# A retention layer feeding a two-layer network: the opening of the kernel written out by hand

## The chip, the cores and the metric
The kernel runs on one core of one Trainium2 chip. The metric is the device time of one execution in microseconds (us), lower is better. Three executions of the kernel before took 356.39, 356.45 and 356.95 us (median 356.45).

## What is computed
For 8 batches of 8 heads, 576 positions and 64 features per head, q, k and v come in as float32. First a retention layer (attention without a softmax, with a decay gamma per head), then two dense layers on 4608 tokens of 512 features:

```python
scores = (q @ k.T) / 8                          # per batch and head, 576 x 576
D[i, j] = gamma[h] ** (i - j) if i >= j else 0
x = (scores * D) @ v                            # heads side by side: 4608 x 512
h = x @ w_in                                    # 512 -> 2048
g = maximum(0.01 * h, h)                        # leaky relu
out = g @ w_out                                 # 2048 -> 512, float32
```

## The kernel before, in words
**Units.** The retention is cut into 40 units: five per batch, four of 128 positions and one of 64. A unit u needs three loads (`load`, L102: k, q and v, 256 KB each, 128 KB for a unit of 64), three casts to f16 (`cast`, L112: k on ACT, q and v scaled by powers of gamma on DVE, v on POOL from some unit on) and then three kinds of TensorE work, which `burst` (L138) issues together:
- `tr`: transposes of q and k (L159), copied out of PSUM as kT (ACT, L249) and qT (DVE or ACT, L250);
- `sc`: the products of k and q within chunks of 64 positions (L171) and the state products k^T v (L184). DVE masks the scores to s16 (L263) and adds the state up over the batch in s32 (L273 to L281, two or three instructions); a copy to f16 is st16 (ACT or POOL, L287);
- `ot`: the output, scores times v (L197) plus state times q (L212), copied to xT by ACT (L257). xT holds the transposed tokens for layer one.

One burst can hold `tr` of unit n, `sc` of unit n-1 and `ot` of unit n-2. Each engine executes its instructions in the order in which this Python code emits them (the schedule is manual), and each waits for its own operands.

**Tokens.** The 4608 tokens are cut into groups (`sizes`, L367): 256, 256, then eight of 512. `g1_blocks` (L388) gives the pieces of layer one of a group. A piece fills one PSUM tile `hps` (two buffers): 4 matmuls of 512 columns, or 8 of 256 in a group of 256, then one leaky relu on ACT (L407). `g2_blocks` (L414) gives layer two: per block of 128 tokens 16 matmuls of 512 columns into a PSUM tile `yps` (two buffers), in four parts of 4; after the last part DVE copies it out (L433) and SP stores it (L435).

**Order.** The units' work is a list of `steps`. `early(u)` (L331, units 0 to 3) casts, issues a burst with `tr` of u and `ot` of u-1, then a second burst with `sc` of u. `steady(n)` (L341) issues loads of unit n+4, then one burst `tr` n, `sc` n-1, `ot` n-2, then the casts of n+1. `run` (L443) emits the pieces of the given lists and spreads the steps between them; `ends[g]` says how many steps must have been emitted before group g. The main part (L454 to L461) emits seven steps up to `steady(5)` first, then layer one of groups 0 and 1 without steps, then layer two of both, two token blocks at a time, with steps 6 to 10 between, then layer one of group 2 with steps 11 to 14, and from there layer one of g alternating with layer two of g-1.

**Queues.** k of unit 0 is loaded through SP. All else in the opening goes through POOL's queue in this order: q and v of unit 0, units 1 to 3, four quarters of w_in (`load_w_in`, cast to f16 by the DMA), unit 4, four quarters of w_out, then units 5 to 8 as the steps come. From unit 9 loads go through SP, in one queue with the stores of the output. t32, the landing buffers of the loads, has five buffers for each of q, k and v.

Of the kernel before, what the change touches and what calls it, by code (L numbers as in the profile page):

```python
# [9 lines left out]
FP = mybir.dt.float32  # L10
# [7 lines left out]
def kernel(  # L18
# [21 lines left out]
    nc = tc.nc  # L40
    B, H, S, D = q.shape
    NT, DM = out.shape
    DFF = moe_w_in.shape[1]
    P = 128
# [3 lines left out]
    NF = DFF // P  # L48
# [24 lines left out]
    o_pool = ctx.enter_context(tc.tile_pool(name="op", bufs=4))  # L73
# [4 lines left out]
    h_pool = ctx.enter_context(tc.tile_pool(name="hpp", bufs=2, space=PSUM))  # L78
    y_pool = ctx.enter_context(tc.tile_pool(name="yp", bufs=2, space=PSUM))
# [13 lines left out]
    w_out16 = const_pool.tile([P, NF, DM], F16, name="w_out16")  # L93

    units = [(b, w) for b in range(B) for w in range((S + P - 1) // P)]
    NU = len(units)
    nrows = [min(P, S - P * w) for b, w in units]
    EARLY = 4
    t32 = {}
    t16 = {}  # L100

    def load(u, x, eng):  # L102
        b, w = units[u]
        n = nrows[u]
        t = ld_pool.tile([P, H, D], FP, name=f"t32_{x}")
        t32[u, x] = t
        eng.dma_start(
            out=t[0:n],
            in_=(q, k, v)[x][b, :, P * w : P * w + n, :].rearrange("h t d -> t h d"),
        )  # L110

    def cast(u, x):  # L112

        b, w = units[u]
        n = nrows[u]
        t = a_pool.tile([P, H, D], F16, name=f"t16_{x}")
        t16[u, x] = t
        if x == 1:
            nc.scalar.copy(out=t[0:n], in_=t32[u, x][0:n])  # L119
        else:  # L120
            eng = nc.gpsimd if (x == 2 and u >= EARLY + 2) else nc.vector
            eng.tensor_tensor(  # L122
                out=t[0:n],
                in0=t32[u, x][0:n],
                in1=tab_sb[0:n, w % 2, x // 2, :].unsqueeze(2).to_broadcast([n, H, D]),
                op=MUL,
            )
# [10 lines left out]
    def burst(tr=None, sc=None, ot=None):  # L138
# [106 lines left out]
        if tr is not None:  # L245
            n = nrows[tr]
            qTs[tr] = a_pool.tile([P, NP, P], F16, name="qT")
            kTs[tr] = a_pool.tile([P, NP, P], F16, name="kT")
            nc.scalar.copy(out=kTs[tr][:, :, 0:n], in_=tiles["tr"][:, 1, :, 0:n])  # L249
            (nc.vector.tensor_copy if tr < EARLY else nc.scalar.copy)(  # L250
                out=qTs[tr][:, :, 0:n], in_=tiles["tr"][:, 0, :, 0:n]
            )
        if ot is not None:
            b, w = units[ot]
            n = nrows[ot]
            t0 = b * S + P * w
            nc.scalar.copy(out=xT[:, :, t0 : t0 + n], in_=tiles["ot"][:, :, 0:n])  # L257
        if sc is not None:
            b, w = units[sc]
            n = nrows[sc]  # L260
            s16 = a_pool.tile([P, NP, 2, CH], F16, name="s16")
            s16s[sc] = s16
            nc.vector.tensor_tensor(  # L263
                out=s16[0:n].rearrange("s p h t -> s (p h) t"),
                in0=tiles["sc"][0:n].rearrange("s p h t -> s (p h) t"),
                in1=mask_sb[0:n].unsqueeze(1).to_broadcast([n, H, CH]),
                op=MUL,
            )
            if n == P:
                st = tiles["st"]  # L270
                s32 = a_pool.tile([P, 2, NP, CH], FP, name="s32")
                if w == 0:
                    nc.vector.tensor_copy(out=s32[:, 0], in_=st[:, 0])  # L273
                else:
                    nc.vector.tensor_tensor(out=s32[:, 0], in0=st[:, 0], in1=carry[b], op=ADD)
                if w % 2 == 0:
                    nc.vector.tensor_tensor(out=s32[:, 1], in0=st[:, 1], in1=s32[:, 0], op=ADD)  # L277
                else:
                    tmp = a_pool.tile([P, NP, CH], FP, name="stmp")
                    nc.vector.tensor_tensor(out=tmp, in0=st[:, 1], in1=s32[:, 0], op=ADD)  # L280
                    nc.vector.tensor_tensor(  # L281
                        out=s32[:, 1], in0=tmp,
                        in1=gblk_sb.unsqueeze(2).to_broadcast([P, NP, CH]), op=MUL,
                    )
                carry[b] = s32[:, 1]
                st16[sc] = a_pool.tile([P, 2, NP, CH], F16, name="st16")
                (nc.scalar.copy if sc < EARLY + 2 else nc.gpsimd.tensor_copy)(  # L287
                    out=st16[sc], in_=s32
                )

# [9 lines left out]
    def load_w_out(c):  # L300
        nc.gpsimd.dma_start(
            out=w_out16[:, 4 * c : 4 * c + 4, :],
            in_=moe_w_out[c * FQ : (c + 1) * FQ, :].rearrange("(c k) f -> k c f", k=P),
        )
# [5 lines left out]
    load(0, 1, nc.sync)  # L310
    load(0, 0, nc.gpsimd)
    load(0, 2, nc.gpsimd)
    for u in range(1, EARLY):
        for x in (1, 0, 2):
            load(u, x, nc.gpsimd)
    for c in range(4):
        load_w_in(c)
    for x in (1, 0, 2):
        load(EARLY, x, nc.gpsimd)
    for c in range(4):  # L320
        load_w_out(c)

    def casts(u):
        if u < NU:
            for x in (1, 0, 2):
                cast(u, x)


    steps = []

    def early(u):  # L331


        def go():
            casts(u)
            burst(tr=u, ot=u - 1 if u else None)
            burst(sc=u)

        steps.append((u - 1, go))

    def steady(n):  # L341
        def go():
            if EARLY + 1 <= n + 4 < NU:
                for x in (1, 0, 2):
                    load(n + 4, x, nc.gpsimd if n + 4 < EARLY + 5 else nc.sync)
            burst(
                tr=n if n < NU else None,
                sc=n - 1 if EARLY <= n - 1 < NU else None,
                ot=n - 2 if EARLY - 1 <= n - 2 else None,
            )  # L350
            casts(n + 1)

        steps.append((n - 2, go))

    def preload():
        for u in range(EARLY + 1, EARLY + 4):
            for x in (1, 0, 2):
                load(u, x, nc.gpsimd)
        casts(EARLY)

    for u in range(EARLY):
        early(u)
    steps.append((EARLY - 1, preload))
    for n in range(EARLY, NU + 2):
        steady(n)

    sizes = [256, 256] + [512] * 8  # L367
    starts = [sum(sizes[:g]) for g in range(len(sizes))]
    NG = len(sizes)
    ends = []  # L370
    for g in range(NG):
        last = max(
            u for u, (b, w) in enumerate(units) if b * S + P * w < starts[g] + sizes[g]
        )
        ends.append(1 + max(i for i, (u, f) in enumerate(steps) if u <= last))
    ends += [ends[-1]] * 2
    done = 0

    def run_steps(upto):
        nonlocal done  # L380
        while done < upto:
            steps[done][1]()
            done += 1

    g_tiles = {}
    y_cur = {}

    def g1_blocks(g):  # L388

        tok, t0 = sizes[g], starts[g]  # L390
        nf = TOK // tok

        def block(fb):
            if fb == 0:
                g_tiles[g] = g_pool.tile([P, NF, tok], F16, name=f"gt{tok}")
            hps = h_pool.tile([P, nf, tok], FP, name="hps")
            for f in range(nf):
                fc = fb * nf + f
                for c in range(NP):
                    nc.tensor.matmul(  # L400
                        out=hps[:, f, :],
                        lhsT=w_in16[:, c, fc * P : (fc + 1) * P],
                        rhs=xT[:, c, t0 : t0 + tok],
                        start=(c == 0),
                        stop=(c == NP - 1),
                    )
            nc.scalar.activation(  # L407
                out=g_tiles[g][:, fb * nf : (fb + 1) * nf, :], in_=hps,
                func=mybir.ActivationFunctionType.Lrelu,
            )  # L410

        return [lambda fb=fb: block(fb) for fb in range(NF // nf)]
# [30 lines left out]
    def run(upto, *lists):  # L443

        order = sorted(
            ((n + 0.5) / len(ls), x, n) for x, ls in enumerate(lists) for n in range(len(ls))
        )
        a = done
        for m, (_, x, n) in enumerate(order):
            lists[x][n]()  # L450
            run_steps(min(upto, a + -(-(upto - a) * (m + 1) // max(1, len(order) - 3)), done + 1))
        run_steps(upto)

    run_steps(ends[1])  # L454
    run(ends[1], g1_blocks(0))
    run(ends[1], g1_blocks(1))
    run(ends[2], g2_blocks(0, 2) + g2_blocks(1, 2))
    run(ends[3], g1_blocks(2))
    for g in range(3, NG):
        run(ends[g + 1], g1_blocks(g), g2_blocks(g - 1))  # L460
    run(ends[NG], g2_blocks(NG - 1))  # L461

# [29 lines left out]
```

## Time and profile before

| | |
|---|---|
| median of three runs | 356.45 us |
| the profiled execution | 356.42 us |
| its span in the profile | 354.4 us |
| PE busy (TensorE matmul) | 306.5 us, 86% |
| ACT busy (ScalarE) | 163.7 us, 46% |
| DVE busy (VectorE) | 112.7 us, 32% |
| POOL busy (GpSimd) | 89.4 us, 25% |
| data moved by DMA | 42.68 MB |

The span runs from the first to the last instruction that the profile shows; the device time holds some two microseconds more. PE busy counts pipelined matmuls by their modelled ends, so the shares are read by stretch, not as a mean.

### The profile page before, as it was taken

How to read it: one execution, taken by the hardware profiler on the slowest of the kernel's cores; microseconds unless marked ns; L12 is line 12 of the kernel's file. 1: busy time of each engine (PE TensorE's matmuls, PEld its weight loads, DVE VectorE, ACT ScalarE, POOL GpSimd, SP SyncE). 2: the span in 40 equal slices, each digit the busy share in tenths (PEclk: the TensorE clock that was granted, in tenths of full speed). 3: DMA queues.
4: the chain of work that ended last, by engine and by line, in shares of the span. 5: the costliest groups of instructions: out<-in, count | busy, mean ns of one | idle time of the engine just before them, and what ended most of it. 6: DMA issues, size and time to landing. Idle time of an engine off the chain costs nothing.

```text
span 354.4 us, 10218 instructions
## 1 busy us (share of the span) xinstructions
PE 306.5 (86%) x4544; PEld 159.7 (45%) x4544; DVE 112.7 (32%) x207; ACT 163.7 (46%) x307; POOL 89.4 (25%) x99
## 2 busy tenths in 40 slices
PE   1342089979889999999999999999999999999995
PEld 1232068544444544444454544444544444444442
DVE  1554030373551343234243424233343321100021
ACT  3233046553776564555465555554465533333300
POOL 8825341043432243022232223221303200000000
PEclk9999999999999999999999999999999999999999
DMA  8999999257995465268075565664620000010011
GB/s 177 213 208 195 222 216 206 62 135 136 225 204 115 103 137 120 76 157 172 32 166 120 135 138 128 125 151 105 153 60 31 31 31 31 30 59 31 30 77 71
DMA packets 98731, 42.68 MB, mean 120 GB/s; under 512 B 88416, under 2 KB 92512, under 8 KB 98688
## 3 DMA queue, kind: packets, MB, share of 16 engines
q1 hardware_dynamic: 92192, 31.33, 38.9%
q0 software_dynamic: 6208, 10.62, 15.8%
q8 instruction: 35, 0.57, 0.7%
q10 hardware_dynamic: 288, 0.08, 0.2%
q14 instruction: 8, 0.07, 0.1%
HBM read 36.78 MB, written 9.44 MB: 130 GB/s over the span
## 4 chain that ended last, share of the span: by engine, by line
PE 81%; DMA 5%; ACT 5%; DVE 4%; issue 3%; POOL 0%; ACTq 0%; POOLq 0%
PE hps L400 34%; PE yps L423 33%; DMA t<-in_q_dram 5%; PE tr L159 4%; PE st L184 3%; PE sc L171 2%; PE ot L197 2%; PE ot L212 2%; ACT t L119 1%; DVE s L263 1%; ACT xT L257 1%; ACT kT L249 1%; DVE t L122 1%; ACT qT L250 1%; ACT gt L407 1%
## 5 line engine op out<-in xcount | busy, mean ns | idle before, releaser
L400 PE MATMUL hps<-xT,w_in 128*128 128x512 f16 (+1 forms) x640 | 145.8, 361 | 2.5 <-ACT gt L407 2.5
L423 PE MATMUL yps<-w_out,gt 128*128 128x512 f16 x576 | 143.7, 379 | 0.0
L407 ACT ACTIVATE gt<-hps 128x512 f16<-128x512 f32 x144 | 86.0, 600 | 95.2 <-PE hps L400 94.2
L400 PEld LDWEIGHTS <-w_in 128*128 128x128 f16 x640 | 61.4, 99 | 61.5 <-issue 3.7
L423 PEld LDWEIGHTS <-gt 128*128 128x128 f16 x576 | 55.2, 98 | 65.0
L287 POOL CAST st<-s 128x512 f16<-128x512 f32 x27 | 26.6, 984 | 175.1 <-DVE s L277 92.1
L159 PE MATMUL tr<-ident,t 64*64 64x64 f16 x1152 | 38.6, 202 | 32.6 <-DVE t L122 31.2
L263 DVE TENSOR_TENSOR s<-sc,cs 128x512 f16<-128x512 f32 (+1 forms) x40 | 27.6, 690 | 104.8 <-PE sc L171 94.0
L433 DVE COPY osb<-yps 128x512 f32<-128x512 f32 x36 | 24.6, 689 | 105.0 <-PE yps L423 105.0
L159 PEld LDWEIGHTS <-t 64*64 64x64 f16 x1152 | 28.7, 114 | 48.9 <-DVE t L122 34.3
L249 ACT COPY kT<-tr 128x512 f16<-128x512 f16 (+1 forms) x40 | 21.7, 542 | 51.7 <-PE sc L171 24.9
L122 DVE TENSOR_TENSOR t<-t,cs 128x512 f16<-128x512 f32 (+1 forms) x46 | 31.2, 685 | 19.9 <-DMA t<-in_q_dram 18.7
L122 POOL TENSOR_TENSOR t<-t,cs 128x512 f16<-128x512 f32 (+1 forms) x34 | 35.1, 1039 | 3.8 <-PE hps L400 2.9
L119 ACT CAST t<-t 128x512 f16<-128x512 f32 (+1 forms) x40 | 25.3, 633 | 11.0 <-DMA t<-in_k_dram 11.0
L171 PE MATMUL sc<-qT,kT 64*64 64x64 f16 x576 | 26.1, 199 | 4.6 <-ACT xT L257 3.4
L197 PE MATMUL ot<-s,t 64*64 64x64 f16 x576 | 24.9, 200 | 1.0
L212 PE MATMUL ot<-qT,st 64*64 64x64 f16 x512 | 24.1, 199 | 0.1
L184 PE MATMUL st<-t,t 64*64 64x64 f16 x512 | 21.2, 204 | 3.2
L257 ACT CAST xT<-ot 128x512 f16<-128x512 f32 (+1 forms) x40 | 22.4, 561 | 1.3 <-PE ot L212 1.3
L171 PEld LDWEIGHTS <-kT 64*64 64x64 f16 x576 | 18.9, 113 | 5.0 <-ACT kT L249 3.3
L250 ACT COPY qT<-tr 128x512 f16<-128x512 f16 (+1 forms) x36 | 19.6, 544 | 0.0
L197 PEld LDWEIGHTS <-t 64*64 64x64 f16 x576 | 17.2, 112 | 2.8 <-issue 2.8
(21 smaller groups left out, 99.6 us busy)
## 6 DMA issues: line engine op xcount, KB each, us to landing
out_dram<-osb SPq DMA_DIRECT2D x36, 256.0 KB, 2.2
t<-in_k_dram SPq DMA_DIRECT2D x25, 256.0 KB, 4.4
t<-in_q_dram SPq DMA_DIRECT2D x24, 256.0 KB, 5.0
t<-in_v_dram SPq DMA_DIRECT2D x24, 256.0 KB, 5.1
t<-in_q_dram POOLq DMA_DIRECT2D x8, 256.0 KB, 8.6
t<-in_v_dram POOLq DMA_DIRECT2D x8, 256.0 KB, 8.5
w_in<-in_moe_w_in_dram POOLq DMA_DIRECT2D x4, 512.0 KB, 12.4
w_out<-in_moe_w_out_dram POOLq DMA_DIRECT2D x4, 512.0 KB, 15.0
```

Source lines behind the costliest of these rows:

```text
L119: nc.scalar.copy(out=t[0:n], in_=t32[u, x][0:n])
L122: eng.tensor_tensor(out=t[0:n], in0=t32[u, x][0:n], in1=tab_sb[0:n, w % 2, x // 2, :].unsqueeze(2).to_broadcast([n, H, D]), op=MUL,)
L159: lambda x=x, p=p, j=j, g=g, hd=hd: nc.tensor.transpose(tiles["tr"][half(g), x, p, half(j)], t16[tr, x][half(j), hd, :], ident[half(j), ha ...
L171: lambda p=p, j=j, g=g, hh=hh: nc.tensor.matmul(out=tiles["sc"][half(j), p, hh, :], lhsT=kTs[sc][half(g), p, half(j)], rhs=qTs[sc][half(g) ...
L184: lambda p=p, j=j, g=g, hd=hd: nc.tensor.matmul(out=tiles["st"][half(g), j, p, :], lhsT=t16[sc, 1][half(j), hd, :], rhs=t16[sc, 2][half(j) ...
L197: lambda p=p, j=j, hh=hh: nc.tensor.matmul(out=tiles["ot"][half(hh), p, half(j)], lhsT=t16[ot, 2][half(j), 2 * p + hh, :], rhs=s16s[ot][ha ...
L212: lambda p=p, j=j, g=g, hh=hh, sx=sx: nc.tensor.matmul(out=tiles["ot"][half(hh), p, half(j)], lhsT=sx[half(g), p, :], rhs=qTs[ot][half(g), ...
L263: nc.vector.tensor_tensor(out=s16[0:n].rearrange("s p h t -> s (p h) t"), in0=tiles["sc"][0:n].rearrange("s p h t -> s (p h) t"), in1=mask ...
L287: (nc.scalar.copy if sc < EARLY + 2 else nc.gpsimd.tensor_copy)(out=st16[sc], in_=s32)
L400: nc.tensor.matmul(out=hps[:, f, :], lhsT=w_in16[:, c, fc * P : (fc + 1) * P], rhs=xT[:, c, t0 : t0 + tok], start=(c == 0), stop=(c == NP ...
L407: nc.scalar.activation(out=g_tiles[g][:, fb * nf : (fb + 1) * nf, :], in_=hps, func=mybir.ActivationFunctionType.Lrelu,)
L423: nc.tensor.matmul(out=y_cur[g, tb], lhsT=g_tiles[g][:, f, tb * P : (tb + 1) * P], rhs=w_out16[:, f, :], start=(f == 0), stop=(f == NF - 1),)
```

## The change
Four units instead of four early steps are written out by hand. The burst of unit n now holds `tr` n, `sc` n-1 and `ot` n-2 from the start, and the pieces of layer one of groups 0 and 1 are emitted by quarters of w_in between the last bursts of the four units and before unit 4 is cast. Layer two of the first four token blocks (`g2_wide`) goes by quarters of w_out over four accumulators (two of `yps`, two borrowed from `hps`), with units 4 to 6 between. Groups are 256, 256, 256, seven of 512, and 256. The loads of units 5 and 6 are queued between quarters of w_out; loads in the steady part are three units ahead instead of four, all through SP. For units 4 to 6 the qT copy moves from ACT to DVE; for units 6 and 7 the st16 copy moves from POOL to ACT and the cast of v from POOL to DVE.

```diff
-    EARLY = 4
+    NFIRST = 7
+    NEARLY = 8
...
-            eng = nc.gpsimd if (x == 2 and u >= EARLY + 2) else nc.vector
+            eng = nc.gpsimd if (x == 2 and u >= NEARLY) else nc.vector
...
-            (nc.vector.tensor_copy if tr < EARLY else nc.scalar.copy)(
+            (nc.vector.tensor_copy if tr < NFIRST else nc.scalar.copy)(
...
-                (nc.scalar.copy if sc < EARLY + 2 else nc.gpsimd.tensor_copy)(
+                (nc.scalar.copy if sc < NEARLY else nc.gpsimd.tensor_copy)(
...
+    for u in (1, 2, 3):
+        loads(u, nc.gpsimd)
     for c in range(4):
         load_w_in(c)
-    for x in (1, 0, 2):
-        load(EARLY, x, nc.gpsimd)
-    for c in range(4):
-        load_w_out(c)
+    load_w_out(0)
+    loads(4, nc.gpsimd)
...
     def steady(n):
         def go():
-            if EARLY + 1 <= n + 4 < NU:
-                for x in (1, 0, 2):
-                    load(n + 4, x, nc.gpsimd if n + 4 < EARLY + 5 else nc.sync)
+            if NEARLY < n + 3 < NU:
+                loads(n + 3, nc.sync)
             burst(
                 tr=n if n < NU else None,
-                sc=n - 1 if EARLY <= n - 1 < NU else None,
-                ot=n - 2 if EARLY - 1 <= n - 2 else None,
+                sc=n - 1 if NFIRST <= n - 1 < NU else None,
+                ot=n - 2 if n - 2 >= NFIRST else None,
             )
             casts(n + 1)
...
-    sizes = [256, 256] + [512] * 8
+    sizes = [256] * 3 + [512] * 7 + [256]
...
-    run_steps(ends[1])
-    run(ends[1], g1_blocks(0))
-    run(ends[1], g1_blocks(1))
-    run(ends[2], g2_blocks(0, 2) + g2_blocks(1, 2))
-    run(ends[3], g1_blocks(2))
-    for g in range(3, NG):
+    def g2_wide(tbs):
+        ys = []
+        def block(part, n):
+            g, tb = tbs[n]
+            for f in range(4 * part, 4 * part + 4):
+                if f == 0:
+                    ys.append(
+                        y_pool.tile([P, DM], FP, name="yps")
+                        if n < 2
+                        else h_pool.tile([P, 1, DM], FP, name="hps")[:, 0, :]
+                    )
+                nc.tensor.matmul(out=ys[n], ...)
+            if part == 3:
+                osb = o_pool.tile([P, DM], FP, name="osb")
+                nc.vector.tensor_copy(out=osb, in_=ys[n])
+                r0 = starts[g] + tb * P
+                nc.sync.dma_start(out=out[r0 : r0 + P, :], in_=osb)
+        return [lambda part=part, n=n: block(part, n) for part in range(4) for n in range(4)]
+
+    def blocks(g, *parts):
+        for fq in parts:
+            for m in (2 * fq, 2 * fq + 1):
+                g1[g][m]()
+
+    g1 = [g1_blocks(g) for g in range(3)]
+    casts(0)
+    burst(tr=0)
+    casts(1)
+    burst(tr=1, sc=0)
+    casts(2)
+    burst(tr=2, sc=1, ot=0)
+    casts(3)
+    burst(tr=3, sc=2, ot=1)
+    blocks(0, 0)
+    burst(sc=3, ot=2)
+    blocks(0, 1)
+    burst(ot=3)
+    blocks(1, 0, 1)
+    blocks(0, 2)
+    blocks(1, 2)
+    for u in (5, 6):
+        loads(u, nc.gpsimd)
+        load_w_out(u - 4)
+    load_w_out(3)
+    for u in (7, 8):
+        loads(u, nc.gpsimd)
+    casts(4)
+    blocks(0, 3)
+    blocks(1, 3)
+
+    wide = g2_wide([(0, 0), (0, 1), (1, 0), (1, 1)])
+    burst(tr=4)
+    casts(5)
+    for m in range(4):
+        wide[m]()
+    burst(tr=5, sc=4)
+    for m in range(4, 7):
+        wide[m]()
+    casts(6)
+    wide[7]()
+    burst(tr=6, sc=5, ot=4)
+    for m in range(8, 11):
+        wide[m]()
+    burst(sc=6, ot=5)
+    for m in range(11, 14):
+        wide[m]()
+    burst(ot=6)
+    for m in range(14, 16):
+        wide[m]()
+    casts(7)
+    loads(9, nc.sync)
+    run(ends[3], g1[2] + g2_blocks(2))
+    run(ends[4], g1_blocks(3))
+    for g in range(4, NG):
         run(ends[g + 1], g1_blocks(g), g2_blocks(g - 1))
     run(ends[NG], g2_blocks(NG - 1))
```

## Rows read from the trace of the kernel before
**Rows 1.** Stretches: us, busy per engine (instructions), clock, DMA share, GB/s
```profile
core 0: us, PE busy (x) PEld busy (x) DVE busy (x) ACT busy (x) POOL busy (x), PEclk, DMA share, GB/s
6.56:47.36 40.80, 12.30 (x432) 9.66 (x432) 15.34 (x29) 9.66 (x19) 22.07 (x28) 1.00 1.16 211
47.36:62.60 15.24, 15.24 (x130) 13.15 (x129) 1.38 (x2) 10.88 (x19) 3.21 (x4) 1.00 1.07 205
62.60:81.60 19.00, 15.67 (x460) 8.66 (x458) 10.23 (x20) 8.88 (x19) 6.00 (x7) 1.00 0.49 114
81.60:110.60 29.00, 25.98 (x481) 12.84 (x482) 11.75 (x22) 19.03 (x37) 9.91 (x10) 1.00 0.90 184
```
**Rows 2.** Timeline of DVE and PE: start, length, line, [idle before <- releaser]
```profile
44.90 0.69 DVE L122 TENSOR_TENSOR t<-t,cs 128x512 f16<-128x512 f32 x1 [13.01 <-DMA t<-in_q_dram]
...
45.65 0.26 PE L159 MATMUL tr<-ident,t 64*64 64x64 f16 x2 [12.83 <-DVE t L122]
...
47.36 14.83 PE L400 MATMUL hps<-xT,w_in 128*128 128x256 f16 x122
```
**Rows 3.** Timeline of POOL: issues of the first and last early load
```profile
1.27 1.05 POOL L107 DMA_DIRECT2D t<-in_q_dram  x1 [0.83 <-POOLq L476]
...
10.20 0.88 POOL L107 DMA_DIRECT2D t<-in_v_dram  x1
```
**Rows 4.** DMA issues of those two, and w_in, w_out by line: us to landing
```profile
t<-in_q_dram POOLq DMA_DIRECT2D x1, 256.0 KB, 4.5
...
t<-in_v_dram POOLq DMA_DIRECT2D x1, 256.0 KB, 7.6
...
L295 POOL DMA_DIRECT2D w_in<-in_moe_w_in_dram x4: 777/778/790, 11.1 to 13.3; - x4
...
DMA to landing us min/median/max: 9.5/12.4/15.5
...
DMA to landing us min/median/max: 14.7/15.0/15.9
```
**Rows 5.** Timeline of ACT and DVE around early unit 1
```profile
13.95 0.58 ACT L249 COPY kT<-tr 128x512 f16<-128x512 f16 x1 [1.24 <-PE tr L159]
...
14.57 0.42 DVE L250 COPY qT<-tr 128x512 f16<-128x512 f16 x1 [1.83 <-ACT kT L249]
16.04 0.69 DVE L263 TENSOR_TENSOR s<-sc,cs 128x512 f16<-128x512 f32 x1 [1.05 <-PE sc L171]
...
17.90 1.29 DVE L122 TENSOR_TENSOR t<-t,cs 128x512 f16<-128x512 f32 x2
...
18.02 0.62 ACT L287 CAST st<-s 128x512 f16<-128x512 f32 x1 [2.99 <-DVE s L281]
18.54 0.61 ACT L119 CAST t<-t 128x512 f16<-128x512 f32 x1
20.42 0.58 ACT L249 COPY kT<-tr 128x512 f16<-128x512 f16 x1 [1.27 <-PE tr L159]
```
**Rows 6.** L400 from 47.36 and from 52, L159 before 35 and from 64: ns min/median/max
```profile
L400 PE MATMUL hps<-xT,w_in x16: 272/421/421, 47.4 to 50.4; 128*128 128x256 f16 x16
...
L400 PE MATMUL hps<-xT,w_in x94: 272/273/273, 51.8 to 61.9; 128*128 128x256 f16 x94
...
L159 PE MATMUL tr<-ident,t x144: 237/238/260, 6.6 to 32.6; 64*64 64x64 f16 x144
...
L159 PE MATMUL tr<-ident,t x144: 192/193/213, 64.5 to 81.3; 64*64 64x64 f16 x144
```
**Rows 7.** Timeline of ACT: xT of unit 3; leaky relus of 256-column pieces two and three
```profile
48.28 0.60 ACT L257 CAST xT<-ot 128x512 f16<-128x512 f32 x1
...
50.66 0.60 ACT L407 ACTIVATE gt<-hps 128x512 f16<-128x512 f32 x1 [0.77 <-PE hps L400]
51.54 0.60 ACT L407 ACTIVATE gt<-hps 128x512 f16<-128x512 f32 x1 [0.28 <-PE hps L400]
```
**Rows 8.** Timeline of DVE: score masks of steps 6 and 10
```profile
65.84 0.69 DVE L263 TENSOR_TENSOR s<-sc,cs 128x512 f16<-128x512 f32 x1 [16.27 <-PE sc L171]
...
81.67 0.68 DVE L263 TENSOR_TENSOR s<-sc,cs 64x512 f16<-64x512 f32 x1 [1.60 <-PE sc L171]
```
**Rows 9.** Chain that ended last: start us, us, what
```profile
91.42 1.02 PE hps L400 x4
96.24 1.02 PE hps L400 x4
...
105.49 4.48 PE hps L400 x20
...
114.67 0.86 PE yps L423 x4
116.70 0.97 PE hps L400 x4
```

More of the change, by code (lines that the diff above doesn't have):

```diff
@@ L312, with loads @@
     load(0, 2, nc.gpsimd)
-    for u in range(1, EARLY):
+    def loads(u, eng):
         for x in (1, 0, 2):
-            load(u, x, nc.gpsimd)
+            load(u, x, eng)
+    for u in (1, 2, 3):
+        loads(u, nc.gpsimd)
     for c in range(4):
         load_w_in(c)
-    for x in (1, 0, 2):
-        load(EARLY, x, nc.gpsimd)
-    for c in range(4):
-        load_w_out(c)
+    load_w_out(0)
+    loads(4, nc.gpsimd)
     def casts(u):
@@ L329 @@
     steps = []
[L331 to L339, printed above, removed]
     def steady(n):
         def go():
-            if EARLY + 1 <= n + 4 < NU:
-                for x in (1, 0, 2):
-                    load(n + 4, x, nc.gpsimd if n + 4 < EARLY + 5 else nc.sync)
+            if NEARLY < n + 3 < NU:
+                loads(n + 3, nc.sync)
             burst(
                 tr=n if n < NU else None,
-                sc=n - 1 if EARLY <= n - 1 < NU else None,
-                ot=n - 2 if EARLY - 1 <= n - 2 else None,
+                sc=n - 1 if NFIRST <= n - 1 < NU else None,
+                ot=n - 2 if n - 2 >= NFIRST else None,
             )
@@ L353, in steady @@
         steps.append((n - 2, go))
[L355 to L364, printed above, removed]
+    for n in range(NFIRST, NU + 2):
         steady(n)
-    sizes = [256, 256] + [512] * 8
+    sizes = [256] * 3 + [512] * 7 + [256]
     starts = [sum(sizes[:g]) for g in range(len(sizes))]
@@ L374 @@
         )
-        ends.append(1 + max(i for i, (u, f) in enumerate(steps) if u <= last))
+        ends.append(sum(1 for u, f in steps if u <= last))
     ends += [ends[-1]] * 2
@@ L452, in run @@
         run_steps(upto)
-    run_steps(ends[1])
-    run(ends[1], g1_blocks(0))
-    run(ends[1], g1_blocks(1))
-    run(ends[2], g2_blocks(0, 2) + g2_blocks(1, 2))
-    run(ends[3], g1_blocks(2))
-    for g in range(3, NG):
+    def g2_wide(tbs):
[9 more added lines that the diff above has]
+                    )
+                nc.tensor.matmul(
+                    out=ys[n],
+                    lhsT=g_tiles[g][:, f, tb * P : (tb + 1) * P],
+                    rhs=w_out16[:, f, :],
+                    start=(f == 0),
+                    stop=(f == NF - 1),
+                )
+            if part == 3:
[4 more added lines that the diff above has]
+        return [lambda part=part, n=n: block(part, n) for part in range(4) for n in range(4)]
```

## The prediction, made before the changed kernel was run
> **What bounds the kernel now.** I read the busy table by stretch first. From 47.36 us on TensorE is nearly always busy; before that it is busy 12.3 of 40.8 us while DMA is saturated (share above 1, 211 GB/s) [rows 1]. So the opening is what can be won. The timeline shows why: unit 5's q is cast only at 44.90, after DVE waited 13.01 us for its load, and TensorE stands 12.83 us before that unit's transposes. Layer one's first matmul comes at 47.36, behind them in TensorE's order [rows 2]. It needed none of this: its tokens are units 0 and 1, and w_in had landed. The first quarter was issued at 11.1 and took 9.5 us (20.6), the last 13.3 + 15.5 = 28.8 [rows 4]. So the wait is one of emission order, not of data.
>
> From 62.60 to 110.60 the losses are smaller: 3.3 and 3.0 us of TensorE idle [rows 1], plus what hides in busy time. There steps follow each other at the pace of their own chain: masks of steps 6 to 10 stand (81.67 - 65.84) / 4 = 3.96 us apart with only 8 matmuls between [rows 8], and 4.82 us apart where three pieces of layer one lie between [rows 9]. Beyond, pieces follow at 0.86 and a burst takes 116.70 - 115.53 = 1.17, plus 0.11 in the matmuls after it [rows 9]. That part I take over as it is.
>
> **The change, part by part.**
> *Loads.* Nothing changes up to w_in. From the first q (1.27 + 4.5 = 5.8) to unit 3's v (10.20 + 7.6 = 17.8) ten loads landed, 1.2 us each [rows 3, 4]; a quarter of w_in took (28.8 - 20.6) / 3 = 2.7. In the new queue order, all on POOL, that gives w_out's first quarter at 31.5, unit 4 33.3, unit 5 36.9, second quarter 39.6, unit 6 43.2, third 45.9, fourth 48.6, unit 7 52.2, unit 8 55.8. POOL has no other work until unit 8's cast, so issuing (0.88 each) costs nothing.
>
> *Four units pipelined.* Today a unit takes 20.42 - 13.95 = 6.47 us, because its second burst stands between the copies and the mask [rows 5]. With one burst per unit the chain is: burst end to kT 0.1, kT 0.6, qT 0.4, then mask to q's cast 17.90 - 16.04 = 1.86, cast 0.65, burst about 1.7 at the early pace: 5.3 us; unit 1 carries one state instruction less and has 4.8. Unit 1's burst starts when its q is cast, load 9.4 plus 0.7, and ends at 11.8; unit 2's ends at 16.7, unit 3's near 22.5. The cast of k still stands behind st16 on ACT (18.02, 18.54 [rows 5]), 0.6 behind q, and stays inside the burst's first half. xT of unit 1 follows kT on ACT, so layer one starts at 23.7 instead of 47.4. w_in's first quarter has been there for 3 us.
>
> *Layer one by quarters.* The first two pieces: 47.36 to 50.6 was 3.3 us for 16 matmuls; the third piece took 0.88 [rows 2, 7]. I charge the slow rate once: 27.0. Burst of unit 3's scores 1.2: 28.2. The last output of unit 3 waits for its mask, three state instructions and st16 (2.8), burst 0.6; its xT stands on ACT behind two leaky relus: the next piece starts at 32.6, with 1.75 us of pieces in those 4.4. Here 2.7 us are lost; the bounds are 0.7 (the xT copy alone shows) and 4.4 (nothing overlaps). Twelve pieces x 0.875 = 10.5: 43.1. Quarters two to four (23.3 to 28.8) are hidden.
>
> *Layer two of four blocks.* Unit 4's transposes 0.8, sixteen parts x 0.865 = 13.8, three bursts x 1.25, the last output burst 0.7 with 0.4 wait for st16 of unit 6: 62.6. The weight quarters and loads arrive 7 us or more ahead of each use. The moves to DVE (three qT, 0.42 each; two casts, 0.69) and to ACT (two st16, 0.62) lie beside these parts; uncovered they would be 3.9 us. The two accumulators borrowed from hps delay group 2's first pieces by at most one DVE copy (0.7): zero taken, since the last output burst and another part lie between.
>
> *Group 2 and steps 7 to 12.* One piece 0.87, step 7 (only transposes) 0.8, two pieces 1.75, step 8 1.2: 67.2. Steps 9 to 12 at the chain's pace, between 3.0 (TensorE's own work) and 4.82: I take 3.8, near the 3.96 row, since two pieces lie between as there. That is 82.4; five parts: 86.7. Unit 9's loads now go through SP behind four stores, the last of which waits for its copy at 63.3; with 1.2 per load they land near 68, needed at 69; units 10 to 12 follow 3.6 apart, against 3.8. Cost taken: zero, bounds 0 and +4.
>
> *Group 3 and steps 13 to 17.* Piece and step 2.1, two periods of 3.8 and two of 4.82 [rows 9], then 2.7 until ACT is free and three pieces: 111.3. Loads three units ahead stay in front by two steps; a load has to wait in SP's queue only for stores already behind it in execution, so I take zero here too.
>
> *The rest.* Five pieces end at 109.97 in the old trace, the last of them group 3's [rows 9]; so at 109.1 the old kernel has layer one of 1024 tokens, layer two of 512 and steps to 14, and needs 245.3 us more to 354.4. At 111.3 the new one has 1280, 768 and 17: 16 pieces (13.8) and three bursts (3.8) less. 245.3 - 17.6 = 227.7. Span 339.0. The new group of 256 tokens at the end adds 0.13 us at most (16 more pieces at 0.875 instead of 0.865). The profiled execution of before took 356.42 with a span of 354.4; the 2.0 around it stay, and 356.42 is at the median (356.45). Forecast 341.0 us, 15.4 less.
>
> **A rule that speaks against it.** The matmuls at 47.4 to 50.4 have 421 ns, those from 52 on 273; transposes 238 before 35 us, 193 from 64 on, although the granted clock reads 1.00 in all these stretches [rows 1, 6]. So the array ran at its lower level, 1.2 GHz, through the thin opening, and rose to 2.4 only under continuous matmuls. The Trainium skill's TensorE: Matmul & The Clock Gate, section "HAM oscillation — how this bites in real kernels", says that short batches of matmuls between waits can send the array back to the half rate each time. The trace speaks for lasting speed once it is up: from 64 to 81 us TensorE waits 3.3 us in pieces of up to 1 us between short bursts, at 193 ns throughout [rows 1, 6].
>
> **Rivals.**
> 1. *The opening runs at half clock (slower than before).* Layer one's pieces and the wide parts from 23.7 to 62.6 at 1.65 and 1.73 instead of 0.87 and 0.865: 14 x 0.78 + 16 x 0.865 = 24.8 us more, 365.8 us. It decides from 18 or 19 of those 30 pieces at half rate (15.4 / 0.82). For it: the opening's rows of 238 ns and three waits of 1 us near 23, 30 and 32. Against: the stretch from 64 on.
> 2. *The quarters bring nothing:* a reader of w_in16 or w_out16 waits for the whole tile. Layer one then starts at 28.8 (+5.1, less the 1 that was waited for anyway near 30), layer two at 48.6 instead of 43.9, of which those 4 are already spent: about +5 in all, 346 us. Against: layer one of group 0 started at 47.36 while xT of unit 3, the same tile, was written only at 48.28 [rows 2, 7]; waits go by region there.
> 3. *Loads become the limit* once unit 9 goes late through SP: DMA lies idle from 55.8 to 63.6, and each of units 9 to 12 comes up to 1 us late: +4, 345 us. For it: 0.2 us of margin per unit; against: the same rate carried steps 11 to 14.
> 4. *The chains overlap better:* mask and q's cast interleave with the load, early bursts already run fast (-1.5), unit 3's last output costs 0.7 (-2), steps come every 3.3 (-4.5): 333 us.
>
> **How the numbers follow.** Forecast 0.50, rival 1 0.06, rival 2 0.13, rival 3 0.16, rival 4 0.15. Predicted 341.0. The forecast's bounds (chain 3.0 to 4.82 in six periods, wait 0.7 to 4.4, loads 0 to 4) give 336 to 347; rivals 2 to 4 carry the range to 333 and 350. A partly slow opening (five pieces, +4) lies inside. About 0.2% (0.7 us) is what can be told from no change. Faster 0.93: everything but rival 1 and what else might eat 15 us; same 0.02; slower 0.05.
>
> **What would show it.** Right: first L400 matmul near 24 us, kT copies of units 1 to 3 about 5 us apart, layer two's first matmul near 44, step 12's mask near 82, and 354.4's equivalent near 339, with TensorE idle before 24 and little after 33. Rival 1 shows as 421 ns matmuls beyond 30 us; rival 2 as a first matmul at 29 and a PE wait on DMA w_in or w_out; rival 3 as waits of DVE or ACT for DMA in_q or in_k at 66 to 82. The forecast is wrong if the first layer-one matmul comes after 30, or if the part from step 18 on takes other than 228 us.

## The result

The changed kernel takes 340.97 us (median of 4 runs, 340.80 to 341.17) against 356.42 us for the one before in the same comparison: ratio 0.9567, 95% interval 0.9550 to 0.9583. The forecast was 341.0 us, with a range of 333 to 350. The profiled execution has a span of 339.0 us; that is the span forecast. All ratios here are of executions in the faster of two states; of the runs below a single execution (348.8 us, with more fillers) fell in the slower one.

By engine the page of the changed kernel shows little: TensorE is busy for about as long as before (306.5 us) in a shorter span.

```profile
PE 308.6 (91%) x4608; PEld 166.4 (49%) x4608; DVE 114.7 (34%) x212; ACT 163.0 (48%) x306; POOL 86.0 (25%) x95
```

The stretches show where the time went; they are cut at the forecast's own points (layer one's first matmul, layer two's first, the end of the wide part, the end of step 12, the end of group 3's layer one). The columns are those of [rows 1].

```profile
6.43:23.37 16.94, 6.83 (x280) 5.60 (x281) 9.40 (x19) 6.12 (x11) 11.38 (x15) 1.00 1.11 211
23.37:43.99 20.62, 19.37 (x241) 15.72 (x241) 4.51 (x9) 12.00 (x21) 11.53 (x14) 1.00 1.16 213
43.99:62.88 18.89, 18.42 (x274) 9.25 (x274) 9.43 (x18) 5.78 (x11) 1.51 (x2) 1.00 0.57 135
62.88:83.43 20.55, 17.45 (x493) 12.58 (x493) 10.52 (x19) 13.45 (x27) 6.15 (x6) 1.00 0.84 190
83.43:111.20 27.77, 25.06 (x502) 12.70 (x502) 14.08 (x27) 19.72 (x39) 11.32 (x12) 1.00 0.98 201
```

The thin opening now ends at 23.37 instead of 47.36 [rows 1], with DMA as full as before (1.11, 211 GB/s): the same loads arrive at the same rate, and TensorE works on what has arrived. Busy for 12.3 of the 40.8 us up to 47.36 before, it is now busy for 19.37 of the 20.62 us from 23.37 on. The chain that ended last of the changed kernel gives the points (start, length, what):

```profile
23.37 3.57 PE hps L383 x16
...
32.38 10.73 PE hps L383 x96
...
43.99 1.83 PE yps L451 x8
...
61.03 1.85 PE hps L451 x8
...
76.34 4.91 DMA t<-in_q_dram
...
83.43 4.42 PE yps L406 x20
...
108.46 3.61 PE hps L383 x16
```

| step of the forecast | forecast | measured |
|---|---|---|
| first matmul of layer one | 23.7 | 23.37 |
| its first two pieces end | 27.0 | 26.94 |
| the twelve pieces start | 32.6 | 32.38 |
| layer two starts | 43.9 | 43.99 |
| wide part ends | 62.6 | 62.88 |
| step 12 ends | 82.4 | 83.43 |
| group 2 ends | 86.7 | 87.85 |
| group 3's layer one ends | 111.3 | 111.2 |
| from there to the end | 227.7 | 227.8 |

The last piece of the x16 row at 108.46 belongs to group 4, as in [rows 9]; hence 111.2. The units run as forecast too. ACT's kT copies of units 1 to 3 stand 5.06 and 5.55 us apart (6.47 in [rows 5]):

```profile
11.64 0.59 ACT L250 COPY kT<-tr 128x512 f16<-128x512 f16 x1 [2.71 <-PE tr L160]
...
16.70 0.59 ACT L250 COPY kT<-tr 128x512 f16<-128x512 f16 x1 [1.47 <-PE tr L160]
...
22.25 0.59 ACT L250 COPY kT<-tr 128x512 f16<-128x512 f16 x1 [1.48 <-PE tr L160]
```

The slow rate at the start of layer one is there as well, once (changed kernel, its line of layer one up to 26.5 us and from 28 us on; ns min/median/max):

```profile
L383 PE MATMUL hps<-xT,w_in x16: 372/417/417, 23.4 to 26.5; 128*128 128x256 f16 x16
...
L383 PE MATMUL hps<-xT,w_in x112: 269/273/283, 28.4 to 42.8; 128*128 128x256 f16 x112
```

### The profile page after: what moved, and what is told of

Same layout as the page of the kernel before. It is cut to its first block, busy times and chain, and to the rows that moved or that the text cites. A ratio compares the mean times of both kernels' runs of the same rounds, so it can differ in the third digit from the quotient of the medians.

```text
span 339.0 us, 10339 instructions
## 1 busy us (share of the span) xinstructions
PE 308.6 (91%) x4608; PEld 166.4 (49%) x4608; DVE 114.7 (34%) x212; ACT 163.0 (48%) x306; POOL 86.0 (25%) x95
## 4 chain that ended last, share of the span: by engine, by line
PE 83%; ACT 6%; DVE 4%; DMA 3%; issue 3%; POOL 1%; ACTq 0%; POOLq 0%
PE hps L383 33%; PE yps L406 32%; PE tr L160 5%; PE st L185 3%; DMA t<-in_q_dram 3%; PE sc L172 2%; PE ot L198 2%; PE hps L451 2%; PE ot L213 2%; PE yps L451 2%; ACT t L120 1%; ACT xT L258 1%; DVE s L264 1%; ACT kT L250 1%; ACT gt L390 1%
## 5 line engine op out<-in xcount | busy, mean ns | idle before, releaser
L406 PE MATMUL yps<-w_out,gt 128*128 128x512 f16 x512 | 128.1, 379 | 0.0
L383 PEld LDWEIGHTS <-w_in 128*128 128x128 f16 x704 | 67.5, 99 | 59.0 <-issue 4.2
L406 PEld LDWEIGHTS <-gt 128*128 128x128 f16 x512 | 49.1, 98 | 56.1
L288 POOL CAST st<-s 128x512 f16<-128x512 f32 x25 | 24.3, 972 | 143.1 <-DVE s L278 79.4
L416 DVE COPY osb<-yps 128x512 f32<-128x512 f32 x32 | 22.1, 690 | 98.6 <-PE yps L406 98.6
L160 PE MATMUL tr<-ident,t 64*64 64x64 f16 x1152 | 37.8, 200 | 18.5 <-DVE t L123 10.9
L160 PEld LDWEIGHTS <-t 64*64 64x64 f16 x1152 | 28.0, 113 | 34.5 <-DVE t L123 21.0
L123 POOL TENSOR_TENSOR t<-t,cs 128x512 f16<-128x512 f32 (+1 forms) x32 | 33.7, 1060 | 28.7 <-DMA t<-in_v_dram 17.2
L123 DVE TENSOR_TENSOR t<-t,cs 128x512 f16<-128x512 f32 (+1 forms) x48 | 32.2, 682 | 9.9 <-DMA t<-in_q_dram 8.6
L198 PEld LDWEIGHTS <-t 64*64 64x64 f16 x576 | 17.0, 111 | 2.9 <-issue 2.3
L251 ACT COPY qT<-tr 128x512 f16<-128x512 f16 (+1 forms) x33 | 18.0, 546 | 0.0
```

Of the source, the lines that this page charges most:

```text
L123: eng.tensor_tensor(out=t[0:n], in0=t32[u, x][0:n], in1=tab_sb[0:n, w % 2, x // 2, :].unsqueeze(2).to_broadcast([n, H, D]), op=MUL,)
L160: lambda x=x, p=p, j=j, g=g, hd=hd: nc.tensor.transpose(tiles["tr"][half(g), x, p, half(j)], t16[tr, x][half(j), hd, :], ident[half(j), ha ...
L198: lambda p=p, j=j, hh=hh: nc.tensor.matmul(out=tiles["ot"][half(hh), p, half(j)], lhsT=t16[ot, 2][half(j), 2 * p + hh, :], rhs=s16s[ot][ha ...
L383: nc.tensor.matmul(out=hps[:, f, :], lhsT=w_in16[:, c, fc * P : (fc + 1) * P], rhs=xT[:, c, t0 : t0 + tok], start=(c == 0), stop=(c == NP ...
L406: nc.tensor.matmul(out=y_cur[g, tb], lhsT=g_tiles[g][:, f, tb * P : (tb + 1) * P], rhs=w_out16[:, f, :], start=(f == 0), stop=(f == NF - 1),)
```

## The experiments

All start from the changed kernel. The theory was: the emission order made TensorE wait for a load that its next work did not need; pipelining and load order only move when that happens.

**Two bursts per unit again.**
```diff
...
-    burst(tr=1, sc=0)
...
-    burst(tr=3, sc=2, ot=1)
+    for u in range(4):
+        casts(u)
+        burst(tr=u, ot=u - 1 if u else None)
+        burst(sc=u)
     blocks(0, 0)
-    burst(sc=3, ot=2)
+    burst(ot=3)
     blocks(0, 1)
-    burst(ot=3)
...
```


> The four first units again take two bursts each (tr of u with ot of u-1, then sc of u), the rest as in the changed kernel; pieces of layer one start after the second burst of unit 3, with ot of unit 3 between the first two quarters. Theory (layer one's place in the order is the gain, the pipelining only brings it forward): first layer-one matmul near 28.7 us instead of 23.4, but unit 3's last output and its xT no longer leave TensorE waiting, so twelve pieces start near 34.3 instead of 32.4: 343.0 us (341.5 to 344.5). Rival (the pipelining of the units is the bulk of the gain): the 5 to 6 us of later start come through in full, 346.5 us or more.

344.4 us (343.3 to 344.8), ratio 0.9652 (0.9624 to 0.9679). Layer one starts at 28.41, 5.0 us late, yet only 2.5 us reach the span (341.5 in the profiled execution, the fastest of the four). The theory holds, at the upper edge of its range: pipelining is worth some 3 of the 15 us.

```profile
28.41 3.53 PE hps L383 x16
33.10 12.42 PE hps L383 x112
```

**Units 4 and 5 ahead of layer one; w_out ahead of unit 5; both.** The first edit is

```diff
-    blocks(0, 0)
     burst(sc=3, ot=2)
-    blocks(0, 1)
     burst(ot=3)
-    blocks(1, 0, 1)
-    blocks(0, 2)
-    blocks(1, 2)
...
     casts(4)
+    burst(tr=4)
+    casts(5)
+    burst(tr=5, sc=4)
+    blocks(0, 0, 1)
+    blocks(1, 0, 1)
+    blocks(0, 2)
+    blocks(1, 2)
...
```
the second
```diff
-    load_w_out(0)
     loads(4, nc.gpsimd)
+    load_w_out(0)
...
-    for u in (5, 6):
-        loads(u, nc.gpsimd)
-        load_w_out(u - 4)
-    load_w_out(3)
-    for u in (7, 8):
-        loads(u, nc.gpsimd)
+    for c in (1, 2, 3):
+        load_w_out(c)
+    for u in (5, 6, 7, 8):
+        loads(u, nc.gpsimd)
```

> Units 4 and 5 (their casts and the bursts tr 4, then tr 5 with sc 4) are emitted before all sixteen pieces of layer one, as in the kernel before; pipelining, load order, wide layer two as in the changed kernel. Theory (emission order made TensorE wait for unit 5's load): TensorE stands idle until unit 5's q is cast near 37, first layer-one matmul near 38.6, sixteen pieces with the slow rate at their start to 54.2, wide part to 71.3 instead of 62.9, of which about 1 us is won back at step 12 where loads were late: 348.5 us (346 to 351). Rival (the order of the pieces does not matter since loads bound the opening anyway): 341 to 343.

> Only the load order of before: unit 4, then four quarters of w_out, then units 5 to 8; emission order of all else as in the changed kernel. Theory (the loads of units 5 and 6 have slack behind layer one): unit 5's q lands near 43.8 instead of 35.7, needed at 47; nothing waits: 341.0 us (340.5 to 341.7). Rival (the load order carries part of the gain): unit 5 8 us later delays its transposes, 343 us or more.

> Both edits at once: units 4 and 5 ahead of layer one, and w_out ahead of unit 5 in the queue. Theory (the two old orders cost only together what before lost: the queue decides when unit 5 lands, the emission order makes TensorE wait for it): first layer-one matmul near 45.8, 7 us behind the run with the emission order alone: 355.5 us (353 to 357.5), nearly the time of before. Rival (the two edits add up independently): the time of the run with the emission order alone plus the difference of the load order alone, so about 348.5.

| | w_out between units (new) | w_out first (old) |
|---|---|---|
| layer one first (new) | 340.97; again 341.56 | 342.0, ratio 0.9586 (0.9561 to 0.9612) |
| units 4, 5 first (old) | 351.1, ratio 0.9847 (0.9792 to 0.9901) | 357.9, ratio 1.0036 (1.0020 to 1.0052) |

The load order is worth nothing that can be told from the second run of the changed kernel while layer one comes first (its 342.0 us lie 0.3 above the range and 1.0 under the rival), and 6.8 us when TensorE has to wait for unit 5. With both old orders the kernel loses all that it gained, pipelining and wide layer two included. The other parts (the copies moved between engines, the sizes of the groups, loads three units ahead) were not undone one by one; by this run they bring nothing without the two orders. The chain shows the wait itself; first units ahead alone, then both edits (the loads named are those of unit 5's q):

```profile
23.59 11.82 DMA t<-in_q_dram
35.43 0.70 DVE t L123
37.95 16.45 PE hps L383 x128
```
```profile
30.99 13.07 DMA t<-in_q_dram
44.08 0.70 DVE t L123
46.60 14.94 PE hps L383 x128
```

Both runs with units first came out 2.5 us above their expectation, just outside their ranges. In the one with units alone first matmul and wide part fit (37.95 for 38.6; the wide part ended at 71.95 for 71.3); with both edits the first matmul was 0.8 late. The 1 us that I wanted back at step 12 was not given back: from the kT copy of step 8 to that of step 12 they take 16.03 and 16.01 us, the changed kernel 15.26, and DVE's cast of q for step 12 waits 0.67 and 0.88 us for its load.

**Is it the clock?** The changed kernel was run again beside the next three.

> The changed kernel unedited, on the chip of the next three runs, so that differences of 1 to 2 us can be told: 341.0 us as before (340.3 to 341.8) by every theory.

341.56 us (341.1 to 341.7), ratio 0.9582 (0.9564 to 0.9599). Then matmuls that nobody reads, in two of TensorE's waits:

```diff
     burst(tr=2, sc=1, ot=0)
+    filler(32)
     casts(3)
     burst(tr=3, sc=2, ot=1)
+    filler(8)
...
+    def filler(count):
+        hps = h_pool.tile([P, P], FP, name="hps")
+        for i in range(count):
+            nc.tensor.matmul(out=hps, lhsT=ident, rhs=ident, start=(i == 0), stop=(i == count - 1))
```


> Adds 40 matmuls of 128 columns on the identity, whose result nobody reads: 32 behind the burst of unit 2, where TensorE waits some 3.5 us for unit 3's cast, and 8 behind the burst of unit 3. Theory (the first two pieces of layer one take 3.57 us instead of 1.75 because the array is at its lower level after a thin stretch): with TensorE kept busy they take 1.75 to 2.2, unit 3's scores come 1.5 us earlier and with them the twelve pieces, 30.9 instead of 32.4: 339.4 us (338.8 to 340.2). Rival (the first pieces are slow for another reason, such as the DMA of w_in into the same memory or the first use of w_in): they stay at 3.5, 341.0 us or, if the added matmuls delay unit 3, up to 342.

339.33 us (338.7 to 339.7), ratio 0.9517 (0.9499 to 0.9536): the best kernel of this study. TensorE's timeline:

```profile
17.13 3.24 PE L476 MATMUL hps<-ident 128*128 128x128 f16 x32
20.58 0.22 PE L160 MATMUL tr<-ident,t 64*64 64x64 f16 x2 [0.21 <-ACT st L288]
...
22.20 0.62 PE L476 MATMUL hps<-ident 128*128 128x128 f16 x8
23.32 1.91 PE L383 MATMUL hps<-xT,w_in 128*128 128x256 f16 x16 [0.50 <-ACT xT L258]
```

32 matmuls of 128 columns in 3.24 us are 1.26 columns a ns, near the 1.2 GHz level; the level rose among them, for each that starts by 19.5 us lasts 314 ns and the last ones 219. After them the first two pieces take 1.91 us instead of 3.57 (3.43 in the second run of the changed kernel), with the same DMA beside them (201 GB/s for 206). So the cause is the array's level and not the first use of w_in. The twelve pieces start at 30.70 instead of 32.18 in that second run, as the theory had it. The profile's granted clock, 1.00 in the whole opening, does not show the level.

**Loads of units 9 to 11 early.** `loads(9, nc.gpsimd)` stands behind `casts(4)`, 10 behind `casts(5)`, 11 behind `casts(6)`, and a step loads unit n+5:

```diff
-            if NEARLY < n + 3 < NU:
-                loads(n + 3, nc.sync)
+            if n + 5 < NU:
+                loads(n + 5, nc.sync)
...
-    loads(9, nc.sync)
```


> Units 9, 10 and 11 are loaded through POOL's queue behind unit 8, as soon as the casts of units 4, 5 and 6 free their buffers, instead of through SP behind the stores of the wide part; from unit 12 on loads go five units ahead instead of three. Theory (DMA stands nearly idle from 52 to 60 us and is then late for steps 9 to 12, where unit 12's q comes 4.9 us after its issue): steps 9 to 12 follow their own chain at 3.4 to 3.6 us instead of 3.8, step 12's burst ends near 82 instead of 83.4: 339.5 us (338.5 to 340.3). Rival (the chain mask, state, cast, burst sets the pace and the load only fills its gap): within 0.4 us of the changed kernel.

> Both edits at once. Theory: the two losses lie one behind the other on TensorE's path, so the gains add, 3.1 us: 337.9 us (337.0 to 339.0). Rival (the earlier opening only waits longer for the loads or chain of units 9 to 12): no better than the better one of the two alone, 339.4.

Early loads alone: 345.2 us (342.4 to 346.1), ratio 0.9665 (0.9632 to 0.9698), slower by a per cent. With the fillers: 339.66 (339.1 to 342.4), ratio 0.9550 (0.9520 to 0.9580), no better than the fillers alone. My theory fell. kT copies of steps 8 and 12 stand 83.44 - 68.18 = 15.26 us apart in the changed kernel and 15.11 here, though no load is waited for any more; the changed kernel, then early loads:

```profile
68.18 0.59 ACT L250 COPY kT<-tr 128x512 f16<-128x512 f16 x1 [0.36 <-PE tr L160]
...
83.44 0.59 ACT L250 COPY kT<-tr 128x512 f16<-128x512 f16 x1 [1.93 <-PE ot L213]
```

```profile
69.50 0.59 ACT L250 COPY kT<-tr 128x512 f16<-128x512 f16 x1 [0.36 <-PE tr L160]
...
84.61 0.59 ACT L250 COPY kT<-tr 128x512 f16<-128x512 f16 x1 [1.73 <-PE sc L172]
```

The chain of mask, state and casts sets that pace; of the 4.91 us of DMA at 76.34 all but 0.2 us filled a gap of it. That is the profiled execution of the first run. In the second run of the same kernel the distance is 15.90, because the cast of q for step 12 waits longer for its load and then, beside POOL's st16 copy (81.43 to 82.04), takes 1.11 us for 0.69:

```profile
81.48 1.11 DVE L123 TENSOR_TENSOR t<-t,cs 128x512 f16<-128x512 f32 x1 [0.51 <-DMA t<-in_q_dram]
```

With w_out first it is 16.84 us (two casts of q wait, 1.25 and 0.51 us). So the loads of units 9 to 12 cost from 0.2 us up, by the execution, and early loads do save that; they lose more elsewhere. The profiled run shows one such loss. POOL's casts of v now stand behind its DMA issues and meet DVE's last state instruction, which takes 1.60 us instead of 0.42 (POOL first, then DVE; in the run with the fillers, last line, 2.99 us):

```profile
58.41 2.05 POOL L123 TENSOR_TENSOR t<-t,cs 128x512 f16<-128x512 f32 x2
...
59.16 1.60 DVE L282 TENSOR_TENSOR s<-stmp,cs 128x256 f32<-128x256 f32 x1
```

```profile
57.68 2.99 DVE L282 TENSOR_TENSOR s<-stmp,cs 128x256 f32<-128x256 f32 x1
```

st16 of unit 6 and the last output burst wait for it. That explains about 1 us of early loads alone. Of the six runs, the four at 345 to 346 us have a mean granted clock of 0.994, the two at 342.4 and 342.5 (the profiled one among them) 0.998. A difference of 0.004 over 343 us would be 2.7 us at half rate, a loss of some 1.4 us (an estimate), in a stretch that no trace here shows; that is at most part of the 3 us between them, the rest is open.

**Layer two block by block; layer one by group.** 
```diff
-        return [lambda part=part, n=n: block(part, n) for part in range(4) for n in range(4)]
+        return [lambda part=part, n=n: block(part, n) for n in range(4) for part in range(4)]
```
and, in a kernel of its own,
```diff
-    blocks(1, 0, 1)
-    blocks(0, 2)
-    blocks(1, 2)
+    blocks(0, 2, 3)
+    blocks(1, 0, 1)
...
-    blocks(0, 3)
+    blocks(1, 2)
     blocks(1, 3)
```


> Layer two of the first four token blocks goes block by block (all four quarters of w_out for one block, then the next) instead of quarter by quarter over four accumulators; the bursts stay between the same numbers of parts. Theory (w_out is ahead of its use by then, so the wide order hides little): the fourth part comes at 46.7 and the last quarter of w_out lands between 45.3 and 47, a wait of 0 to 0.5 us: 341.8 us (341.2 to 342.5). Rival (the wide order is needed because w_out arrives in quarters): TensorE waits 2 us or more for w_out, 343.5 us or more.

342.46 us, ratio 0.9601 (0.9584 to 0.9619), at the upper edge of the range; the changed kernel had 0.9567 and 0.9582, so the difference is not clear of them. The trace shows the one wait for w_out, 0.96 us instead of the 0 to 0.5 expected:

```profile
48.02 1.02 PE L451 MATMUL yps<-w_out,gt 128*128 128x512 f16 x4 [0.96 <-DMA w_out<-in_moe_w_out_dram]
```

> After the last output of unit 3, layer one finishes group 0 (quarters three and four) before it starts group 1, instead of going on with group 1's first quarters. Theory (two losses of the opening lie on xT of unit 3, which group 0 does not read): pieces resume as soon as ACT has emptied a PSUM tile, near 31.4 instead of 32.4, and w_in's last quarter (28.8) is there: 340.7 us (340.0 to 341.4). Rival (the pause is ACT's two leaky relus behind st16, not xT): no change, 341.5 us.

340.40 us, ratio 0.9544 (0.9526 to 0.9562): in the range, but unclear against the changed kernel's first 0.9567. The mechanism held in part. The pieces resume at 32.02 (32.18 in the changed kernel's second run, 32.38 in its first), not at 31.4; but layer one also starts later here, and from its start the pieces come after 8.27 us (8.51 and 9.01). TensorE's wait of 0.67 us for xT is gone:

```profile
32.02 10.68 PE hps L383 x96
```

What was overlooked is that the pieces stand behind unit 3's last output in TensorE's order; that output waits for st16, which ends at 31.16, and ends itself at 32.0.

**More fillers.** Alone, and together with layer one by group:
```diff
     burst(tr=0)
+    filler(12)
...
     burst(tr=1, sc=0)
+    filler(28)
...
     burst(tr=2, sc=1, ot=0)
+    filler(60)
...
     burst(tr=3, sc=2, ot=1)
+    filler(16)
```

> Matmuls on the identity that nobody reads fill TensorE's waits between all four units: 12 behind the burst of unit 0, 28 behind unit 1, 60 behind unit 2, 16 behind unit 3. Theory (the lower level also stretches the bursts of units 2 and 3, some 0.3 us each): layer one starts near 22.8 and its first two pieces take 1.9 us: 338.8 us (338.2 to 339.6), 0.5 below the run with 40. Rival (the units' pace is set by DVE and ACT, the clock only counts in the first two pieces): 339.3 us, like the run with 40; if a filler overruns a cast, up to 340.

> The fillers between all four units and layer one by group, together. Theory (both shorten the same path one behind the other): 338.0 us (337.2 to 338.9). Rival (with the fillers the pause after unit 3's last output is set by st16 and the leaky relus alone, so the group order has nothing left to give): 338.8 us or the same as the fillers alone.

344.5 us (342.9 to 348.8), ratio 0.9646 (0.9623 to 0.9668), and 342.7 (342.6 to 344.4), ratio 0.9624 (0.9602 to 0.9646): both slower than with 40 fillers; both theories and rivals missed. In the first TensorE stood 2.60 us in unit 2's burst for nothing that the profile shows, the granted clock fell to 0.50 in this wait (0.84 on average from 16.6 to 19.3 us), and the 60 fillers took 6.24 us, ahead of unit 3's burst; at the upper level 8 took 0.62 and 16 took 1.07, by which 60 would take some 3.5 (an estimate). Layer one started at 28.03 instead of 23.32. Its timeline, then stretches:

```profile
19.35 0.26 PE L172 MATMUL sc<-qT,kT 64*64 64x64 f16 x2 [2.60 <-issue]
19.55 6.24 PE L476 MATMUL hps<-ident 128*128 128x128 f16 x60
```
```profile
15.00:17.00 2.00, 1.47 (x89) 1.02 (x87) 0.67 (x2) 0.92 (x3) 1.18 (x2) 1.00 1.04 208
17.00:20.00 3.00, 0.65 (x7) 0.58 (x8) 0.77 (x2) 0.79 (x2) 1.38 (x2) 0.74 1.22 201
20.00:22.00 2.00, 2.00 (x22) 2.00 (x20) 1.93 (x5) 0.37 (x1) 0.24 (x1) 0.50 1.25 207
22.00:24.00 2.00, 2.00 (x21) 2.00 (x20) 0.80 (x2) 0.77 (x2) 0.74 (x2) 0.50 1.23 208
```

What the 2.60 us were is open. A second such wait, of 1.86 us, stands in layer one, and the run with both edits has the two as well (2.10 and 1.43):

```profile
31.30 1.86 issue
33.16 1.81 PE hps L383 x15
```

One packet of the instruction queue runs at 16 to 17 us; but so it does in the changed kernel and with 40 fillers, where TensorE has no such wait there.

## Why the prediction was right

*Emission order.* Right, and shown by the two-by-two table: the old place of units 4 and 5 costs 10 us with the new load order and 16 with the old one (357.9 against 342.0).

*Pipelined units.* Right to 0.25 us (5.06 and 5.55 us for the 4.8 and 5.3 forecast); undone, it costs about 3 us, not the 5 by which layer one is late, since unit 3's last output then has its st16 in time. The path was another one. The forecast let q's cast on DVE start the burst and k's cast end inside its first half. The chain goes through ACT, st16 and then k's cast, and the burst, begun at 14.72, has to wait for k:

```profile
14.10 0.62 ACT st L288
14.72 0.53 ACT t L120
...
15.29 0.26 PE tr L160 x2
```

The gap in the burst is about the 0.25 us. That layer one came so near 23.7 owes something to a slip: the forecast put the end of unit 3's burst near 22.5, where its own 16.7 + 5.3 give 22.0; it ended at 22.2.

*Slow rate charged once.* Right, and its cause is shown by the fillers. Rival 1 did not come: after 28 us the matmuls have 273 ns. But a fall back to half rate, which the forecast weighed and set aside by the stretch from 64 us on, is real: with more fillers the granted clock went from 1.00 to 0.50 in a wait of 2.6 us.

*Loads hidden.* Right for w_in, w_out and units 5 to 8: TensorE waits for none of them. For w_out the order by quarters is needed for that, though for 0.96 us only. Rival 2 is refuted: layer one started at 23.37, while w_in's last quarter landed at 28.7 (issue 13.3, 15.4 to landing).

*Steps 9 to 12.* 15.3 us for 15.2 forecast. Step 12 ended 1.0 late, and nearly all of it was there before step 9: the wide part ended 0.3 late, step 7 waited 0.4 for a cast behind DVE's copy of the output, its transposes and the two pieces behind them took 0.3 more than charged; step 8 waited for nothing.

```profile
62.90 0.69 DVE osb L460
63.59 0.61 DVE t L123
...
64.24 0.44 PE tr L160 x16
```

Rival 3 (+4 us) did not come, but its waits are not free, and the forecast's zero for them is a little low: without a wait for a load steps 9 to 12 take 15.1 us, with w_out by blocks as with early loads, so the loads cost 0.2 us in the profiled execution and 0.8, the slower cast included, in that of the second run.

*Group 3.* 23.4 us for 24.6 forecast: periods of two and three pieces were 3.3 to 3.6 and 4.4 to 4.6 us instead of 3.8 and 4.82. Rival 4 came here and nowhere else: this is 1.2 of its 8 us. It cancels the 1.1 us by which group 2 ended late. That the sum hit to a tenth is luck; that each stage lies within 1.3 us is not. The range tells less: its bounds, added up, give 334.2 to 352.8 and not 336 to 347, and none of rivals 2 to 4 lies above 346, where the range goes to 350.

## What to carry to other kernels

Where engines take their work in order, ask of the first instruction behind a long wait which data it needs itself; if they were there, the gain is the wait, and the way to it is a different place in the order. What a load order is worth depends on the emission order: about nothing here with the new one, 6.8 us with the old. Undo each alone and then both. A gap in DMA is a loss only as far as some chain waits for it at its end, here 0.2 to 0.8 us; filling it cost more, in part because the issues stood ahead of POOL's casts.

## What the hardware showed that I had not expected

- DVE and POOL collide on instructions whose operands all lie in SBUF: DVE's 0.42 us multiply took 1.60 and 2.99 us, and ended 0.3 us after POOL's two casts did. The Trainium skill's SBUF — State Buffer, section "SBUF: two separate sides", says so: a DVE instruction with two SBUF inputs and a GpSimd instruction that reads SBUF hold a shared port pair exclusively, and the loser waits out the whole instruction. The 1.60 us agree as far as POOL's first cast began 0.75 us ahead of DVE's instruction; DVE waited out both casts. The 2.99 us do not follow from it: there DVE's instruction began 0.65 us ahead of the casts, beside a DMA issue of POOL, and still ended behind them.
- 40 matmuls that nobody reads, 3.9 us of TensorE time inside its waits, gave 2.2 us back; 116 took 3 away.
- The granted clock reads 1.00 through an opening in which matmuls run at the 1.2 GHz pace, and 0.50 at 20 to 24 us of the run with more fillers. Only the matmuls' own spacing tells the first case.
